# Issuing both loads of the Q and K weights from ScalarE's queue in a four-layer kernel

## The chip, the cores and the metric

The kernel runs on one core of one Trainium2 chip. The metric is the device time of one execution in microseconds (us). A core has five engines with an instruction queue each: TensorE (PE, with its weight loads as PEld), VectorE (DVE), ScalarE (ACT), GpSimd (POOL) and SyncE (SP). SyncE computes nothing; in this kernel its queue issues all transfers (DMAs).

## The reference

The input x has 2048 tokens of 512 features in bf16. Four layers follow each other, A, B, A, B, with the same weights for both A and both B. Each takes a layernorm of x and adds its result to x.

```
x = x + A(layernorm(x))      # linear attention, 32 heads of 16
x = x + B(layernorm(x))      # relu(x @ w1) @ w2, 512 -> 1376 -> 512
x = x + A(layernorm(x))
x = x + B(layernorm(x))

A:  q, k, v = x @ wqkv                      # 512 -> 3 * 512
    pq, pk = phi(q), phi(k)                 # phi(t) = (t + 1 if t > 0 else exp(t)) + 1e-6
    kv = sum over tokens of pk * v, z = sum over tokens of pk
    o = (pq @ kv) / (pq . z + 1e-6),  result = o @ wo
```

## The kernel before

The 2048 tokens are 16 tiles of 128 tokens, four tiles to a chunk. Weights and activations stay in on-chip memory; x is read once into `xin` and the result written once. Every operation is an entry of a graph (`g.add`, and `dma` for a transfer). A planner (`_list_schedule`) walks the graph with estimated costs and hand-made priorities (`HINTS`, `SEQS`) and gives each engine a fixed order. `emit_engine` then writes each engine's instructions in that order, with a semaphore wait for every dependence that is not known to be met already. A transfer is always an entry of SP's order, and the engine that needs its data waits for the transfer's own semaphore to reach 16.

What the change touches is the start of the first layer. SP's order there is:

- `ld_x0_0`: tile 0 of x, 128 KB, one run of 1 KB for each of 128 partitions (line 744)
- `ld_x0_1`: tiles 1 to 3 of x, 384 KB, one run of 3 KB for each partition (line 744)
- `ld_wqk0`: the Q and K columns of rows 0 to 255 of wqkv, 512 KB, two runs of 2 KB for each partition (line 750)
- `ld_wqk1`: the same of rows 256 to 511, 512 KB (line 750)
- `ld_x1_0` and `ld_x1_2`: tiles 4 and 5, and 6 and 7, of x, 256 KB each; the second is issued only when `ld_x0_1` has landed
- chunks 3 and 2 of x, 512 KB each, in that order; chunk 3 is issued only when `ld_wqk1` has landed

None of the first five waits for anything. PE begins with matmuls on constants (`warm`, line 775) whose results nobody reads. Tiles 0 to 3 then take a short path: VectorE computes the statistics (lines 802 and 803), subtracts the mean (line 1554), PE transposes the tile (line 883), and ScalarE or VectorE copies the transposed tile to `Tb` (lines 887 and 888). Two further statistics, those of tile 3, are made by ScalarE (lines 1564 and 1566), in front of its first copies. The K projections and the token-wise Q projections of these four tiles (line 928, `wqkv` and `Tb`) are split into a part a over rows 0 to 255, which needs `ld_wqk0`, and a part b over rows 256 to 511, which needs `ld_wqk1`. From chunk 1 on a tile is normalized on VectorE (line 845) and transposed by a DMA (line 866, `Tb<-xn`). ScalarE evaluates a projection in two passes (lines 910 and 912), VectorE finishes it (lines 914 and 921).

ScalarE's own order begins with `table` (lines 763 and 765): it loads a function table and runs a tiny activation that reads `nhalf`, which POOL sets (line 783). The function that the diff edits:

Of the kernel before, what the change touches and what calls it, by code (L numbers as in the profile page):

```python
# [606 lines left out]
def build_kernel(nc, A_x, A_wqkv, A_wo, B_w1, B_w2, out, n_layers_pairs=2, A_PE_CHUNKS=0, windows=None,  # L607
# [20 lines left out]
    with es:  # L628
# [52 lines left out]

        sem_eng = {e: es.enter_context(nc.semaphore("sem_" + e)) for e in (PE, ACT, DVE, POOL)}
        dma_sems = []

        g = _Graph()
        eng_h = {PE: nc.tensor, ACT: nc.scalar, DVE: nc.vector, POOL: nc.gpsimd, SP: nc.sync}
# [21 lines left out]
        def dma(emit, reads, writes, xfer_ns, name, issue=C_SP_ISSUE, late=0.0):  # L708
            sem = es.enter_context(nc.semaphore("dsem%d" % len(dma_sems)))
            dma_sems.append(sem)  # L710

            def _emit(eng, emit=emit, sem=sem):
                return emit(eng).then_inc(sem, 16)
            op = g.add(SP, _emit, reads, writes, dur=issue, lat=xfer_ns, dma=True, name=name)
            op.seq = sem
            op.late = late
            return op
# [25 lines left out]
        def ld_x(t, lo=0, hi=4, lat=1300.0, after=()):  # L743
            dma(lambda e: e.dma_start(xin[:, 4 * t + lo:4 * t + hi, :], tok_view(A_x, t, lo, hi)),  # L744
                list(after), [("xin", i) for i in range(4 * t + lo, 4 * t + hi)], lat, "ld_x%d_%d" % (t, lo))
# [3 lines left out]
        for k in range(2):  # L749
            dma(lambda e, k=k: e.dma_start(wqkv[:, 2 * k:2 * k + 2, 0:2 * D], wq_v[:, 2 * k:2 * k + 2, 0:2 * D]),  # L750
                [], [("wk", k), ("wq", k)], 1700.0, "ld_wqk%d" % k, late=(0.0, 300.0)[k])
# [109 lines left out]
        def transpose_chunk(t, extra_reads=(), parts=1):  # L861
            n = 4 // parts
            for k in range(parts):
                i0 = 4 * t + n * k
                lat = 2650.0 if parts == 1 else (2350.0 if k == 0 else 1050.0)
                dma(lambda e, i0=i0: e.dma_start_transpose(Tb[:, i0:i0 + n, :, :].rearrange("p i c t -> p (i c) t"),
                                                           xn[:, i0:i0 + n, :].rearrange("p i d -> p (i d)")),
                    [("xn", i) for i in range(i0, i0 + n)] + list(extra_reads),
                    [("T", i) for i in range(i0, i0 + n)], lat, "tr%d_%d" % (t, k), issue=1300.0)
# [946 lines left out]
        def emit_engine(e, handle):  # L1816
            for o in order[e]:
                for d in waits[o.idx]:
                    if d.dma:
                        handle.wait_ge(d.seq, 16)  # L1820
                    else:
                        handle.wait_ge(sem_eng[d.eng], d.seq)  # L1822
                ins = o.emit(handle)
                if not o.dma:
                    ins.then_inc(sem_eng[e], 1)
            if e == SP:
                for o in final_waits:
                    handle.wait_ge(o.seq, 16)

        with nc.Block() as block:  # L1830
            @block.tensor
            def _(t):
                emit_engine(PE, t)

            @block.scalar
            def _(s):
                emit_engine(ACT, s)

            @block.vector
            def _(v):  # L1840
                emit_engine(DVE, v)

            @block.gpsimd
            def _(p):
                emit_engine(POOL, p)

            @block.sync
            def _(sp):
                emit_engine(SP, sp)
# [3 lines left out]
def bass_interleave_layers__linear_attn_block__dense_activation_relu__prompt_kernel(  # L1853
    nc: bass.Bass,
    A_x: bass.AP,
    A_wqkv: bass.AP,
    A_wo: bass.AP,
    B_x: bass.AP,
    B_w1: bass.AP,
    B_w2: bass.AP,  # L1860
    out: bass.AP,
):
    build_kernel(nc, A_x, A_wqkv, A_wo, B_w1, B_w2, out)
# [28 lines left out]
```

## Time and profile before

| | |
|---|---|
| median of 3 runs | 267.29 us (267.24 to 267.83) |
| the profiled execution | 267.75 us |
| its span, first to last instruction | 266.0 us |
| granted TensorE clock, mean | 1.000 |
| PE busy | 260.9 us, 98% of the span |
| DVE, ACT, POOL busy | 215.4, 192.0, 51.2 us |
| DMA queues | one for data (q1), two for instructions |

The page of the profile gives one execution. Times of instructions are in us from the start of the span; the span leaves out some 1.75 us that the measured time of that execution has around it. A timeline row has the start, the length, the engine, the line, the operation, output and input, the count of merged instructions, and in brackets the idle time before the first of them with what ended it.

### The profile page before, as it was taken

The numbers are of one execution on the slowest core, as the hardware profiler recorded it, in microseconds if no ns is written. First come the engines' busy times: TensorE is split into PE (matmuls) and PEld (weight loads), VectorE is DVE, ScalarE is ACT, GpSimd is POOL, SyncE is SP. The second block draws the span as 40 slices with busy tenths as digits, with TensorE's granted clock in tenths as the row PEclk, the third lists the DMA queues.
The fourth block names the chain that finished last, engine by engine and source line by source line (L and its number), as shares of the span: only waits on it lengthen the run. The fifth ranks groups of instructions, "written<-read, shape, count | busy, mean of one in ns | idle before, by whom it ended". The sixth has DMA issues, their size and how long they took to land.

```text
span 266.0 us, 5120 instructions
## 1 busy us (share of the span) xinstructions
PE 260.9 (98%) x1890; PEld 171.2 (64%) x1890; DVE 215.4 (81%) x557; ACT 192.0 (72%) x420; POOL 51.2 (19%) x131
## 2 busy tenths in 40 slices
PE   7999999999999999999999999999999999999996
PEld 3344444644755888767776744474488888888874
DVE  4897986799889999879786848479999888697865
ACT  4798899998975756898718689578599974656300
POOL 6410010012860023400001340001734040000000
PEclk9999999999999999999999999999999999999999
DMA  6744489866249023150000313054460501602104
GB/s 213 252 88 81 139 159 366 229 156 100 44 87 160 0 21 58 25 99 1 2 0 0 66 27 68 4 140 111 107 120 2 99 2 38 140 2 70 52 1 160
DMA packets 48122, 23.22 MB, mean 87 GB/s; under 512 B 38784, under 2 KB 45920, under 8 KB 48096
## 3 DMA queue, kind: packets, MB, share of 16 engines
q1 hardware_dynamic: 48096, 22.88, 37.2%
q8 instruction: 15, 0.25, 0.4%
q14 instruction: 11, 0.09, 0.1%
HBM read 7.14 MB, written 2.10 MB: 35 GB/s over the span
## 4 chain that ended last, share of the span: by engine, by line
PE 91%; DMA 4%; DVE 3%; SPq 1%; issue 0%; DVEq 0%
PE ps L928 91%; DMA xin<-in_A_x_dram 3%; DMA Tb<-xn 1%; DVE bst L802 1%; DVE big L921 1%; DVE xn L845 0%; DVE wqkv L944 0%; SPq L750 0%; SPq L744 0%; DVE escr L914 0%; DVE xn L1610 0%; DVE mv L803 0%; DVE veps L809 0%; DVEq L1822 0%
## 5 line engine op out<-in xcount | busy, mean ns | idle before, releaser
L928 PE MATMUL ps<-Tb,w 128*128 128x256 f16 (+2 forms) x240 | 42.0, 301 | 0.0
L1327 ACT ACTIVATE big<-ps 128x512 bf16<-128x512 f32 x58 | 33.0, 597 | 10.3 <-PE ps L928 10.0
L960 ACT ACTIVATE sqscr<-xres 128x512 bf16<-128x512 f32 x48 | 29.9, 626 | 9.6 <-DVE xres L954 9.4
L928 PE MATMUL ps<-w,big 128*128 128x256 bf16 (+5 forms) x213 | 36.5, 293 | 0.0
L928 PE MATMUL ps<-wqkv,Tb 128*128 128x512 bf16 x144 | 34.5, 379 | 0.9 <-DMA wqkv<-in_A_wqkv_dram 0.6
L928 PE MATMUL ps<-big,xn 128*128 128x512 bf16 (+1 forms) x160 | 31.2, 336 | 0.2 <-DVE veps L809 0.2
L910 ACT ACTIVATE big<-ps 128x512 bf16<-128x512 f32 x48 | 28.7, 603 | 1.5 <-PE ps L928 1.4
L928 PEld LDWEIGHTS ps<-Tb,w 128*128 128x128 f16 (+1 forms) x240 | 23.2, 98 | 9.3
L928 PE MATMUL ps<-xn,xin 128*128 128x256 f16 x168 | 28.8, 272 | 0.0
L1274 DVE TENSOR_TENSOR ps<-ps,escr 128x256 f32<-128x256 f32 x56 | 22.8, 427 | 7.1 <-PE ps L928 6.6
L912 ACT ACTIVATE escr<-ps 128x512 bf16<-128x512 f32 x44 | 25.7, 604 | 3.4 <-PE ps L928 3.3
L928 PE MATMUL ps<-Tb,wqkv 128*128 128x512 bf16 x112 | 27.1, 379 | 0.0
L825 POOL TENSOR_SCALAR mean<-s 128x4 f32<-128x4 f32 (+1 forms) x13 | 3.7, 285 | 117.4 <-DVE xres L954 117.3
L928 PE MATMUL ps<-Mf,big 128*128 128x512 bf16 x112 | 25.0, 379 | 0.0
L928 PEld LDWEIGHTS ps<-wqkv,Tb 128*128 128x128 bf16 x144 | 13.7, 98 | 16.5 <-DMA wqkv<-in_A_wqkv_dram 1.1
L928 PEld LDWEIGHTS ps<-w,big 128*128 128x128 bf16 (+1 forms) x213 | 20.3, 98 | 5.2
L928 PEld LDWEIGHTS ps<-big,xn 128*128 128x128 bf16 x160 | 15.1, 98 | 12.1 <-POOL xn L979 0.7
L928 PE MATMUL ps<-xin,big 128*128 128x256 bf16 x150 | 20.8, 272 | 0.0
L914 DVE TENSOR_SCALAR escr<-escr 128x512 bf16<-128x512 bf16 x52 | 14.3, 286 | 6.7 <-ACT escr L912 6.5
L928 PEld LDWEIGHTS ps<-Mf,big 128*128 128x128 bf16 x112 | 10.7, 98 | 12.7 <-DVE big L1105 0.3
L921 DVE TENSOR_TENSOR big<-big,escr 128x512 bf16<-128x512 bf16 x46 | 18.4, 417 | 0.2
L928 PEld LDWEIGHTS ps<-Tb,wqkv 128*128 128x128 bf16 x112 | 10.8, 98 | 11.7 <-issue 0.4
(139 smaller groups left out, 499.4 us busy)
## 6 DMA issues: line engine op xcount, KB each, us to landing
big<-rdc SPq DMA_DIRECT2D x32, 128.0 KB, 2.7
wqkv<-in_A_wqkv_dram SPq DMA_DIRECT2D x3, 512.0 KB, 5.0
w<-in_B_w_dram SPq DMA_DIRECT2D x1, 1376.0 KB, 7.6
w<-in_B_w_dram SPq DMA_DIRECT2D x1, 1280.0 KB, 10.8
xin<-in_A_x_dram SPq DMA_DIRECT2D x2, 512.0 KB, 4.5
out_dram<-wqkv SPq DMA_DIRECT2D x2, 512.0 KB, 3.5
xin<-in_A_x_dram SPq DMA_DIRECT2D x2, 256.0 KB, 6.2
wo<-in_A_wo_dram SPq DMA_DIRECT2D x1, 512.0 KB, 7.6
```

The lines of the kernel that those rows point to most:

```text
L802: g.add(DVE, lambda e: e.bn_stats(bst[:, i, :], xin[:, i, :]), [("xin", i)] + list(after), [("bst", i)], C_DVE_BNST, name="bnst%d" % i)
L825: g.add(POOL, lambda e: e.tensor_scalar(mean[:, sl], s1[:, sl], -INV_D, None, ALU.mult), [("s1", i) for i in tl], [("mean", i) for i in tl ...
L910: g.add(ACT, lambda e: e.activation(dst_ap, psv[:, b, :], ACTF.Identity, bias=1.0 + 1e-6, scale=sc), [("ps", b)] + rk, [dst_key], C_ACT_PS ...
L912: g.add(ACT, lambda e: e.activation(esc, psv[:, b, :], ACTF.Exp, scale=sc), [("ps", b)] + rk, [ekey], C_ACT_EXP + xd, name=name + "_exp")
L914: g.add(DVE, lambda e: e.tensor_scalar(esc, esc, 1.0, 1e-6, ALU.min, ALU.add), [ekey], [ekey], C_DVE_BF4X, name=name + "_em")
L921: g.add(DVE, lambda e: e.tensor_tensor(dst_ap, dst_ap, esc, ALU.max), [dst_key, ekey], [dst_key], 340.0, name=name + "_phi")
L928: last = e.matmul(o, l, r, start=st, stop=sp, skip_group_check=skip)
L960: g.add(ACT, lambda e: e.activation(sqscr[:, q, :], xres[:, i, :], ACTF.Square, accum_out=s2[:, i:i + 1]), [("xres", i)], [("sqscr", q), ( ...
L1274: g.add(DVE, lambda e: e.tensor_tensor(psv[:, bank, 256:512], psv[:, Y, 0:256], m5, ALU.add), [("ps", Y), ("escr", s)], [("ps", bank)], C_ ...
L1327: g.add_flex([(ACT, lambda e: e.activation(unit_ap(u), psv[:, b, :], ACTF.Relu), C_ACT_PSUM), (DVE, lambda e: e.tensor_scalar(unit_ap(u), ...
```

## The change

`ld_wqk0` and `ld_wqk1` stay in SP's order as entries that emit no instruction. Their two DMA instructions are written at the head of ScalarE's queue, in front of its function table load. Each still increments its own semaphore, so whoever waits for the weights does so as before, and so do SP's later loads. The order of every engine's other operations is unchanged.

```diff
--- before.py
+++ after.py
@@ -681,6 +681,8 @@
         dma_sems = []
+        ACT_LOADS = ('ld_wqk0', 'ld_wqk1')
+        act_loads = []
 
@@ -711,6 +713,9 @@
             def _emit(eng, emit=emit, sem=sem):
                 return emit(eng).then_inc(sem, 16)
+            if g.layer == 0 and name in ACT_LOADS:
+                act_loads.append((ACT_LOADS.index(name), _emit))
+                _emit = lambda eng: None
             op = g.add(SP, _emit, reads, writes, dur=issue, lat=xfer_ns, dma=True, name=name)
@@ -1834,6 +1839,8 @@
             @block.scalar
             def _(s):
+                for _, load in sorted(act_loads, key=lambda a: a[0]):
+                    load(s)
                 emit_engine(ACT, s)
```

## The prediction

> **What bounds the kernel now.** I read the page first, then the waits of PE, then the first 20 us of each queue's timeline, since the change touches nothing later.
>
> ```profile
> span 266.0 us, 5120 instructions
> PE 260.9 (98%) x1890; PEld 171.2 (64%) x1890; DVE 215.4 (81%) x557; ACT 192.0 (72%) x420; POOL 51.2 (19%) x131
> ...
> PE ps L775 <- PEq L1877: 0.8, 1, 0.8
> PE ps L883 <- DVE xn L1554: 0.6, 1, 0.6
> PE ps L928 <- DMA wqkv<-in_A_wqkv_dram: 0.6, 1, 0.6
> PE ps L928 <- DMA Tb<-xn: 0.3, 1, 0.3
> PE ps L928 <- DVE veps L809: 0.2, 1, 0.2
> ```
>
> PE is the bound, and the five rows are all of its waits in the whole execution. Where they lie, the timelines show; first PE, then DVE:
>
> ```profile
> 0.83 3.78 PE L775 MATMUL ps<-const-bfloat16-1.0 128*128 128x512 bf16 x9 [0.83 <-PEq L1877]
> 4.41 0.42 PE L883 MATMUL ps<-ident,xn 128*128 128x128 bf16 x2
> ...
> 6.01 0.40 PE L883 MATMUL ps<-ident,xn 128*128 128x128 bf16 x4 [0.63 <-DVE xn L1554]
> ...
> 7.77 0.59 PE L928 MATMUL ps<-wqkv,Tb 128*128 128x512 bf16 x2
> 8.96 5.79 PE L928 MATMUL ps<-wqkv,Tb 128*128 128x512 bf16 x26 [0.60 <-DMA wqkv<-in_A_wqkv_dram]
> 14.95 3.19 PE L928 MATMUL ps<-big,xn 128*128 128x512 bf16 x16 [0.20 <-DVE veps L809]
> ...
> 20.65 1.90 PE L928 MATMUL ps<-wqkv,Tb 128*128 128x512 bf16 x8 [0.35 <-DMA Tb<-xn]
> ...
> 2.88 0.69 DVE L802 BATCH_NORM_STATS2 bst<-xin 128x6 f32<-128x512 bf16 x1 [2.88 <-DMA xin<-in_A_x_dram]
> ...
> 4.66 0.70 DVE L802 BATCH_NORM_STATS2 bst<-xin 128x6 f32<-128x512 bf16 x1 [0.47 <-DMA xin<-in_A_x_dram]
> ...
> 7.99 0.42 DVE L888 COPY Tb<-ps 128x512 bf16<-128x512 bf16 x1
> 9.58 1.29 DVE L802 BATCH_NORM_STATS2 bst<-xin 128x6 f32<-128x512 bf16 x2 [1.18 <-DMA xin<-in_A_x_dram]
> ```
>
> After the warm-up, which reads no data, PE works on tiles 0 to 3, waits 0.60 us for the second half of the weights at 8.96, and then 0.20 and 0.35 us more, at 14.95 and 20.65. The last two are fed by the normalization of chunk 1, which starts at 9.58, when VectorE has stood idle for 1.18 us for `ld_x1_0`. So two landings hold the start back, the weights' at 8.96 and chunk 1's at 9.56; behind 20.65 PE never waits. The chain of work that ended last goes the second way: SP's issues, one behind the other, then that load, VectorE, the DMA transpose, and PE for 242 us.
>
> ```profile
> 1.71 0.43 SPq L750
> 2.13 0.04 issue
> 2.18 0.47 SPq L750
> 2.65 0.04 issue
> 2.69 6.87 DMA xin<-in_A_x_dram
> ...
> 16.75 3.86 DMA Tb<-xn
> 20.61 0.05 issue
> 20.65 242.27 PE ps L928 x1790
> ```
>
> **What the edit moves.** Two issues of 0.43 and 0.47 us leave SP's queue, and with their gaps `ld_x1_0` is issued 0.98 us earlier, at about 1.71. SP's issue of `ld_x1_2` hangs on `ld_x0_1`, and chunk 3 and then chunk 2 on `ld_wqk1`; these follow their releasers, and nothing near the start waits for them. On ScalarE the two issues come first:
>
> ```profile
> 0.79 0.87 SPq L744 DMA_DIRECT2D xin<-in_A_x_dram  x2
> ...
> 2.62 1.28 ACT L763 ACT_TABLE_LOAD   x1 [2.62 <-POOL nhalf L783]
> 3.92 0.20 ACT L765 ACTIVATE lnw<-nhalf 128x2 f32<-128x2 f32 x1
> 4.66 0.63 ACT L1564 ACTIVATE sqscr<-xin 128x512 bf16<-128x512 bf16 x1 [0.54 <-DMA xin<-in_A_x_dram]
> ```
>
> If ScalarE's queue starts like SP's, at 0.79, the 0.90 us of issues end at 1.7, and the table load waits for POOL until 2.62 anyway: cost nothing. Without that cover there is still the 0.54 us in front of 4.66. `ld_wqk1` is issued at some 1.26 instead of 2.18, 0.92 us earlier; `ld_wqk0` also 0.92.
>
> **The price.** The first x loads had the transfer engines to themselves for their first microsecond; now the weights start beside them. The windows of one microsecond (PE, PEld, DVE, ACT and POOL busy, PE clock, DMA share, GB/s):
>
> ```profile
> 1.00:2.00 1.00, 1.00 (x3) 0.29 (x2) 0.00 (x0) 0.00 (x0) 0.94 (x2) 1.00 0.15 44
> 2.00:3.00 1.00, 1.00 (x4) 0.38 (x3) 0.12 (x1) 0.38 (x1) 0.60 (x3) 1.00 1.02 225
> 3.00:4.00 1.00, 1.00 (x4) 0.35 (x3) 0.93 (x3) 0.99 (x2) 0.12 (x1) 1.00 1.05 290
> 4.00:5.00 1.00, 1.00 (x7) 0.61 (x6) 0.53 (x2) 0.46 (x2) 1.00 (x3) 1.00 0.78 272
> ...
> 6.00:7.00 1.00, 0.99 (x11) 0.67 (x11) 0.97 (x3) 0.81 (x4) 0.84 (x4) 1.00 0.99 381
> 7.00:8.00 1.00, 1.00 (x9) 0.50 (x8) 0.96 (x5) 0.81 (x3) 0.91 (x4) 1.00 1.00 387
> ```
>
> Call D the delay of `ld_x0_1`, on whose landing both VectorE and ScalarE start at 4.66. By 4.65 44 + 225 + 290 + 0.65 x 272 = 736 KB had moved. The two x loads are 128 and 384 KB, 524 thousand bytes; the other 212 KB were weights already. At the full rate of 384 KB per us (the last two rows), the 2.65 us from 2.0 to 4.65 could have moved 1018 KB and moved 692, so 326 KB were spare. No run here shows two load queues side by side (all data went by one), so I bound D:
> - None: if the weights only fill the spare capacity.
> - 0.81 us: if the two queues take turns run by run and nothing spare can be used. The x loads have 256 runs (one per partition and load), `ld_wqk0` has 256, so all of it, 524 KB, goes ahead of the last x run, 312 KB more than now, over 384.
> - 1.24 us: if besides that the two queues issue one at a time, so that `ld_x0_1` waits for one issue of 0.43.
> - 2.18 us: if all 1049 KB of weights go first, (1049 - 212) / 384.
>
> I take 0.6, the middle of the first and the third. The dips at 225 to 290 GB/s are those of loads that have just begun and would in part recur. Tile 0 may be delayed as much; its short chain had 0.47 us of slack in front of 4.66, so D decides.
>
> On the arbitration the Trainium skill ("DMA: Bandwidth & Descriptors", section on queues, rings and completion order) says that each transfer engine serves its queues in turn, a packet at a time, which would give about the second value; no run here shows it yet. The same page ("Issuing engines are not separate DMA queues") speaks against the edit: several issuing engines save only the time to issue. The 0.90 us of the rows above is that time, and the transfer rate is no higher.
>
> **The sum.** PE's work on tiles 0 to 3 and everything up to 8.96 shifts by D; the waits of 0.60 + 0.20 + 0.35 = 1.15 us go. Shift of the end: 0.6 - 1.15 = -0.55. The same through VectorE: it is done with the first tiles at 8.41, now 9.01, and starts chunk 1 at 9.01 in place of 9.58, 0.57 earlier; the feeds of 14.95 and 20.65 come that much earlier. That needs `ld_x1_0` landed by 9.01 (9.56 less 0.98 of issue is 8.58) and `ld_wqk1` by about 8.80: the two matmuls at 7.77 take 0.22 us each, 5.79 over 26, so PE is ready at 8.20 plus D. It is there at 8.96 now, and comes at about 8.0 if the transfers follow the issue. Both hold with half a microsecond or so to spare; they are what is late next. A lead of PE survives behind 20.65, where ScalarE too waits for PE:
>
> ```profile
> 21.73 0.60 ACT L910 ACTIVATE big<-ps 128x512 bf16<-128x512 f32 x1 [0.44 <-PE ps L928]
> ```
>
> The profiled execution took 267.75 us, 1.75 beyond its span, and 0.46 above the median of the three runs, 267.29. Against its own time the sum gives 267.20, against the median 266.7, which I forecast.
>
> **The rivals.** One of them needs a row of the first 9.5 us by line and shape (busy time, mean ns of one):
>
> ```profile
> L775 PE MATMUL ps<-const-bfloat16-1.0 128*128 128x512 bf16 x8 | 3.6, 625 | 0.8 <-PEq L1877 0.8
> ```
>
> - A larger gain: D near zero. For it speaks the spare 326 KB against 312 KB needed; against it, the dips. -1.15 us: 266.1.
> - No change: D of 0.9 to 1.6, because the two queues' issues exclude each other and share what is left; -0.25 to +0.45 us, about 267.4. For it: even the plain alternation gives 0.81. The Trainium skill ("Perfetto Trace Analysis", the DMA instruction on HWDGE) has one descriptor generator, locked by one queue at a time, and would give the third value of D, near 267.4; no run here shows whether ScalarE's issues are held up by SP's.
> - Slower, by the weights first: they are the older or longer work on each transfer engine and x comes behind them, D = 2.18, shift +1.03, 268.3. It decides against the edit from D = 1.15 on. For it: x has only 128 KB queued when the weights' 512 KB arrive. Against: SP's first issue is no later than ScalarE's.
> - Slower, by a cold PE: the warm-up ends at 4.61, and the first transpose, at 4.41 now, comes D or more later, so PE stands idle for over half a microsecond where it now runs through. The eight warm-up matmuls of 512 columns took 3.6 us, 0.45 each, and those behind 8.96 take 0.22, so PE starts at half speed and speeds up only after some 4 us of work. If the gap puts this off by a few microseconds, the eight projections up to 8.4 cost 8 x 0.23 = 1.84 more, the 16 transposes at twice their cost some 0.9; 0.63 of it goes into the wait at 6.01. 0.6 + 2.1 - 1.15 = +1.55, half that much extra +0.5; I price it at +1.0, 268.3. Against it: over 3.5 us of unbroken warm-up stay as they were. By the Trainium skill ("TensorE: Matmul & The Clock Gate", Part 1) the clock rises after a busy window of about 3.4 us; by that the warm-up nearly suffices alone, if the window lies well.
>
> **How the numbers follow.** The forecast's case, D of 0.3 to 0.9 and so -0.85 to -0.25 us, gets 0.40; the larger gain 0.12; no change 0.14; weights first 0.16; the cold PE 0.18. What a measurement of this kernel can tell from no change is about 0.2%, 0.53 us. Of the forecast's case 0.26 lies beyond that and 0.14 within; of no change 0.10 lies within and 0.04 is slower when a landing is late besides. Faster: 0.26 + 0.12 = 0.38. Same: 0.14 + 0.10 = 0.24. Slower: 0.16 + 0.18 + 0.04 = 0.38. The range goes from 266.1, the larger gain, to 268.4, just past the price of both slow cases; it leaves out the long tails of these two, somewhat under 0.2. The forecast's own range is 266.4 to 267.0.
>
> **What would show it.** Right: a second data queue in the profile; the weights' issues at the head of ScalarE's queue, before 1.8; VectorE's first statistics later than 2.88 and its second at about 5.3; no wait of PE at the second half of the weights, which begins at about 8.8; no wait of VectorE for `ld_x1_0`; PE's 0.20 and 0.35 gone, and the long stretch of PE beginning near 20.1. Wrong: second statistics at 6 or later (weights first); transposes spaced twice as far and projections at 0.45 us behind 5 us (cold PE); issues of ScalarE and SP that alternate (one generator); or waits of PE for `wqkv` or `Tb` as long as before.

## The result, and the profile after

| | before | after |
|---|---|---|
| median | 267.70 us of 9 executions (267.10 to 268.44) | 269.51 us of 9 executions (268.28 to 271.01) |
| ratio, 95% interval | | 1.0072 (1.0055 to 1.0089) |
| the profiled execution, its span | 267.75, 266.0 us | 269.59, 267.9 us |

The change makes the kernel slower by 0.72%; the medians differ by 1.8 us. The kernel before has 267.70 here and had 267.29 in the three runs ahead of the prediction, so 0.4 us of the distance to the forecast is that of the base. The page of the profile after (span 267.9 us), its line of busy times, PE's waits and the two data queues (packets, MB, share of the transfer engines' span):

```profile
PE 261.9 (98%) x1890; PEld 172.0 (64%) x1890; DVE 215.6 (80%) x557; ACT 191.8 (72%) x420; POOL 50.9 (19%) x131
...
q1 hardware_dynamic: 47552, 21.83, 35.9%
q10 hardware_dynamic: 544, 1.05, 1.2%
...
PE ps L888 <- DVE xn L1559: 2.3, 1, 2.3
...
PE ps L933 <- DMA Tb<-xn: 0.3, 1, 0.3
```

All lines stand five higher than before (L928 is L933 now). The waits for `wqkv` and for `veps` are gone, as intended. In their place stands one wait of 2.3 us for a normalized tile, and PE is busy 1.0 us longer with the same 1890 instructions. The timelines of ScalarE, VectorE and PE:

```profile
0.79 0.99 ACTq L755 DMA_DIRECT2D wqkv<-in_A_wqkv_dram  x2
2.62 1.28 ACT L768 ACT_TABLE_LOAD   x1 [2.62 <-POOL nhalf L788]
...
3.06 0.69 DVE L807 BATCH_NORM_STATS2 bst<-xin 128x6 f32<-128x512 bf16 x1 [3.06 <-DMA xin<-in_A_x_dram]
6.12 0.69 DVE L807 BATCH_NORM_STATS2 bst<-xin 128x6 f32<-128x512 bf16 x1 [1.76 <-DMA xin<-in_A_x_dram]
10.90 0.42 DVE L893 COPY Tb<-ps 128x512 bf16<-128x512 bf16 x1 [1.36 <-PE ps L888]
...
7.48 0.60 PE L888 MATMUL ps<-ident,xn 128*128 128x128 bf16 x4 [2.33 <-DVE xn L1559]
8.52 1.91 PE L933 MATMUL ps<-wqkv,Tb 128*128 128x512 bf16 x4
```

ScalarE's two issues are done at 1.78 and cost its table load nothing. Tile 0's statistics begin 0.18 us later than before (3.06 against 2.88). Those of tile 1, which need `ld_x0_1`, begin at 6.12 in place of 4.66: 1.46 us later. PE then stands idle from 5.15 to 7.48. Its first four projections at 8.52 take 1.91 us in all. The same four of before took 1.13:

```profile
6.58 1.13 PE L928 MATMUL ps<-wqkv,Tb 128*128 128x512 bf16 x4
```

The windows of after (columns as in the prediction) show why:

```profile
6.00:7.00 1.00, 0.00 (x0) 0.00 (x0) 0.84 (x2) 0.88 (x3) 0.00 (x0) 1.00 1.00 389
7.00:8.00 1.00, 0.52 (x5) 0.52 (x6) 0.96 (x4) 0.72 (x3) 0.80 (x2) 0.74 0.92 316
8.00:9.00 1.00, 1.00 (x8) 0.66 (x7) 0.93 (x4) 0.88 (x3) 0.83 (x5) 0.50 0.15 55
10.00:11.00 1.00, 1.00 (x8) 0.59 (x6) 0.10 (x1) 0.00 (x0) 0.18 (x1) 0.55 0.87 336
```

The granted clock, full since 4.08, falls to 0.50 at 7.50 and is back at 10.91, 3.4 us after each. Ahead of 4.08 the trace has no entry of the clock, and the view prints 1.00 there, as in the prediction's rows; that PE starts at half speed shows in the length of its matmuls alone. For the same reason the mean granted clock of an execution leaves out a late first rise (it is 1.000 for one below whose clock rises at 9.81). The clock at half explains the projections' length and VectorE's wait of 1.36 for PE at 10.90. The chain that ended last names the late load, and where PE's unbroken stretch begins:

```profile
1.25 4.85 DMA xin<-in_A_x_dram
...
22.49 242.27 PE ps L933 x1790
```

The stretch is 242.27 us long in before as well and begins 1.84 us later than there (20.65). The times of the two executions differ by 1.84 too. So here all of the loss arises before 22.5 us, and from here on I follow that beginning, called S.

### The profile page after: what moved, and what is told of

Read it like the earlier page. It is cut to its first block, busy times and chain, and to the rows that moved or that the text cites. A ratio compares the mean times of both kernels' runs of the same rounds, so it can differ in the third digit from the quotient of the medians.

```text
span 267.9 us, 5120 instructions
## 1 busy us (share of the span) xinstructions
PE 261.9 (98%) x1890; PEld 172.0 (64%) x1890; DVE 215.6 (80%) x557; ACT 191.8 (72%) x420; POOL 50.9 (19%) x131
## 4 chain that ended last, share of the span: by engine, by line
PE 92%; DMA 3%; DVE 2%; ACT 1%; issue 0%; SPq 0%; DVEq 0%
PE ps L933 91%; DMA xin<-in_A_x_dram 2%; DMA Tb<-xn 1%; PE ps L888 1%; DVE bst L807 0%; DVE xn L850 0%; ACT big L915 0%; DVE big L926 0%; DVE wqkv L949 0%; DVE escr L919 0%; ACT escr L917 0%; SPq L749 0%; DVE xn L1559 0%; DVE mv L808 0%; DVE xn L1615 0%
## 5 line engine op out<-in xcount | busy, mean ns | idle before, releaser
L933 PE MATMUL ps<-Tb,w 128*128 128x256 f16 (+2 forms) x240 | 42.0, 301 | 0.0
L933 PE MATMUL ps<-w,big 128*128 128x256 bf16 (+5 forms) x213 | 36.5, 293 | 0.0
L933 PE MATMUL ps<-wqkv,Tb 128*128 128x512 bf16 x144 | 35.2, 387 | 0.3 <-DMA Tb<-xn 0.3
L933 PE MATMUL ps<-big,xn 128*128 128x512 bf16 (+1 forms) x160 | 31.2, 336 | 0.0
L933 PEld LDWEIGHTS ps<-Tb,w 128*128 128x128 f16 (+1 forms) x240 | 23.1, 98 | 9.3
L933 PE MATMUL ps<-xn,xin 128*128 128x256 f16 x168 | 28.8, 272 | 0.0
L933 PE MATMUL ps<-Tb,wqkv 128*128 128x512 bf16 x112 | 27.1, 379 | 0.0
L933 PE MATMUL ps<-Mf,big 128*128 128x512 bf16 x112 | 25.0, 379 | 0.0
L933 PEld LDWEIGHTS ps<-wqkv,Tb 128*128 128x128 bf16 x144 | 14.2, 100 | 15.8 <-DMA Tb<-xn 0.6
L933 PEld LDWEIGHTS ps<-w,big 128*128 128x128 bf16 (+1 forms) x213 | 20.3, 98 | 5.2
L933 PEld LDWEIGHTS ps<-big,xn 128*128 128x128 bf16 x160 | 15.2, 98 | 11.7 <-issue 0.7
L933 PE MATMUL ps<-xin,big 128*128 128x256 bf16 x150 | 20.8, 272 | 0.0
L933 PEld LDWEIGHTS ps<-Mf,big 128*128 128x128 bf16 x112 | 10.7, 97 | 12.7 <-DVE big L1110 0.3
L933 PEld LDWEIGHTS ps<-Tb,wqkv 128*128 128x128 bf16 x112 | 10.8, 98 | 11.7 <-issue 0.4
```

The source lines that it names most:

```text
L933: last = e.matmul(o, l, r, start=st, stop=sp, skip_group_check=skip)
```

## The experiments

The reading above gives two joint causes: the weights' first load, issued before `ld_x0_1`, is served ahead of it, and the gap that this makes on PE lets the clock fall. Rivals: that the second queue itself costs, whatever the order; that the clock alone costs; that the gain expected was there only in the one execution profiled. What follows from each run is told by mechanism, not by the letters that some expectations use.

**The same order of loads from one queue.** Before, with `ld_wqk0` in front of `ld_x0_1` on SP's queue; ScalarE issues nothing:

```diff
+        order[SP][1], order[SP][2] = order[SP][2], order[SP][1]
```

> The kernel before, all loads from SP's queue, with only the issues of the second load of x and the first weights' load exchanged (x tile 0, weights 0, x tiles 1 to 3, weights 1). Theory A (what matters is which transfer goes first, not which queue issues it): the second load of x lands at 6.1 to 6.5 us in place of 4.65, PE is idle for 2 us or more in front of tile 2, the clock falls as in the changed kernel, and the time is 1.5 to 2.5 us over the kernel before. Rival B (the second queue itself is what costs, by its ring or its issue): less than 0.7 us over the kernel before, the delay less the waits that go.

269.98 us, ratio 1.0081 (1.0062 to 1.0099). Timelines of SP's queue, VectorE and PE:

```profile
1.25 0.41 SPq L750 DMA_DIRECT2D wqkv<-in_A_wqkv_dram  x1
1.71 0.46 SPq L744 DMA_DIRECT2D xin<-in_A_x_dram  x1
...
5.99 0.69 DVE L802 BATCH_NORM_STATS2 bst<-xin 128x6 f32<-128x512 bf16 x1 [1.64 <-DMA xin<-in_A_x_dram]
7.35 0.40 PE L883 MATMUL ps<-ident,xn 128*128 128x128 bf16 x4 [2.17 <-DVE xn L1554]
22.40 1.90 PE L928 MATMUL ps<-wqkv,Tb 128*128 128x512 bf16 x8 [0.32 <-DMA Tb<-xn]
```

One queue with that order does what the change does with two: `ld_x0_1` at 5.99, a wait of 2.17, S at 22.40. In five of the six executions the mean granted clock is 0.993 or 0.994. The order is enough for the whole loss, and the second queue isn't needed for it.

**Half of the change.** Only `ld_wqk0` goes to the head of ScalarE's queue:

```diff
-        ACT_LOADS = ('ld_wqk0', 'ld_wqk1')
+        ACT_LOADS = ('ld_wqk0',)
```

> Half of the change: only the first weights' load is the first instruction of ScalarE's queue, the second stays on SP's queue at 1.71 us behind the second load of x. Theory A (loads are served whole in the order of issue): the first weights' load, issued at 0.79, is ahead of the second load of x, which lands at 5.6 to 6.2 as in the changed kernel, and the time is that of the changed kernel, 1 to 2 us over the kernel before. Rival B (both weights' loads crowd x out together): the second load of x lands by 5.2 and the time is within 0.5 us of the kernel before.

269.82 us, ratio 1.0072 (1.0049 to 1.0095): all of the loss. The profiled execution is one of the shorter ones, 268.42. Timelines of VectorE and PE, and PE's busy time in the 3.41 us behind the rise of the clock:

```profile
6.00 0.69 DVE L807 BATCH_NORM_STATS2 bst<-xin 128x6 f32<-128x512 bf16 x1 [1.53 <-DMA xin<-in_A_x_dram]
7.92 1.12 PE L933 MATMUL ps<-wqkv,Tb 128*128 128x512 bf16 x4
21.02 1.90 PE L933 MATMUL ps<-wqkv,Tb 128*128 128x512 bf16 x8 [0.53 <-DMA Tb<-xn]
...
5.81:9.22 3.41, 1.87 (x18) 1.17 (x19) 3.08 (x9) 2.97 (x8) 1.98 (x7) 1.00 0.92 299
```

Here `ld_x0_1` is as late as in the swap, but the clock rose only at 5.81 and kept its height, and S is 21.02 in place of 22.40. So by this one profile the late load alone costs some 0.7 us (21.0 against 20.3, the mean of three profiles of before, below) and the fall of the clock 1.3 to 1.4 more. The six executions fall apart accordingly: 268.05 and 268.42 with a mean granted clock of 1.000, and four of 269.75 to 269.96, three of them with 0.994 (the fourth has 1.000).

**The gap filled.** The change, with eight (then five) more warm-up matmuls of 512 columns in front of tile 2's transposes. A second line, not shown, holds the planner's estimate of that entry at its old value:

```diff
-                warm([256], "warm%d" % k)
+                warm([256] + ([512] * 8 if k == 5 else []), "warm%d" % k)
```

> The changed kernel, with eight warm-up matmuls of 512 columns on constants more in front of tile 2's transposes, where PE stood idle from 5.15 to 7.48 us. Theory A (two costs: the first weights' load goes ahead of the second load of x, which lands 1.46 us later than before; and PE's idle stretch lets the granted clock fall to 0.50 from 7.5 to 10.9 us): the loads land as in the changed kernel (VectorE's second statistics at about 6.1 us), the clock stays at 1.00, and only the delay less the waits that go is left, 0.3 to 0.5 us over the kernel before, about 1.5 us under the changed kernel. Rival B (the clock costs nothing here, the late load alone makes the 1.8 us): no faster than the changed kernel, 1.5 to 2 us over the kernel before.

> The changed kernel with five (instead of the eight of the first experiment) warm-up matmuls of 512 columns more in front of tile 2's transposes. At half speed they take 5 x 0.43 = 2.1 us and at full speed 1.1, so they end before the late tile arrives in either case. Theory A (PE's idle stretch costs through the clock, in those executions in which the clock's window falls on it; the eight of before also delayed PE where the clock was still low, and moved a code fetch onto a DMA transpose): the time falls below the changed kernel's 269.5 to some 268.0 to 268.8, and no execution shows a mean clock of 0.994. Rival B (the clock is not what spreads the changed kernel's times): 269.3 or more, as with eight.

269.31 us, ratio 1.0068 (1.0047 to 1.0089), with eight; 268.98, 1.0060 (1.0041 to 1.0078), with five. PE's timeline with eight:

```profile
20.57 1.90 PE L933 MATMUL ps<-wqkv,Tb 128*128 128x512 bf16 x8 [0.33 <-DMA Tb<-xn]
68.10 1.70 PE L933 MATMUL ps<-Tb,w 128*128 128x256 bf16 x13 [0.83 <-DMA Tb<-xn]
```

and with five:

```profile
20.98 1.90 PE L933 MATMUL ps<-wqkv,Tb 128*128 128x512 bf16 x8 [0.33 <-DMA Tb<-xn]
68.37 0.83 PE L933 MATMUL ps<-Tb,w 128*128 128x256 bf16 x6 [0.70 <-DMA Tb<-xn]
```

At the start both do what the clock's part demands: it stays up (in none of the twelve executions is its mean below 0.999), and S is 20.57 and 20.98, though `ld_x0_1` comes at 5.71 and 6.14. But the time follows only in part. By its median the first fits the rival, that the clock costs nothing; the second lies between the two forecasts. Both profiled executions have a wait that before and after don't have, 0.83 and 0.70 us for a DMA transpose near 68. That is about half of the 1.75 us by which the first one's median exceeds before's, and its profiled execution, 268.75, is the shortest of six; what the longer ones, up to 270.36, had is not on record. Two fetches of instructions, on q8 and q14, lie in that stretch. The DMA queues (packets, MB, share of the transfer engines' time) of the eight-matmul kernel from 65 to 66 us:

```profile
q14 instruction: 1, 0.01, 10.6%
q8 instruction: 1, 0.02, 5.8%
```

and of before, from 65 to 66 and from 68 to 69:

```profile
q14 instruction: 1, 0.01, 3.1%
...
q8 instruction: 1, 0.02, 5.7%
```

With the extra PE instructions both fetches fall into the microsecond in which the chunk's two transposes are under way, and these land 5.6 us after their issue (the mean of the two) in place of 3.6. In before the larger fetch comes when they have landed. I read the wait as the fetches' from where they lie; no run takes them away, so this is not shown. The medians can't price the clock, but the beginnings of the stretch do.

**A cold start without the change.** Before, with one of the eight leading warm-up matmuls of 512 columns (the ninth, of 256, stays, so two of nine are left):

```diff
-                    for n in cols:
+                    for n in cols[-1:]:
```

> The kernel before with one of its nine leading warm-up matmuls instead of nine (PE idle until the first transpose at about 4.2 us); all loads as before. Theory A (PE's clock follows its activity, and with the kernel's first projections at half speed the start of PE's unbroken stretch moves): projections near 7 us take 0.43 each instead of 0.22, the unbroken stretch begins at 21.5 to 23 us in place of 20.65, and the time is 1 to 2.5 us over the kernel before, with no transfer changed. Rival B (the clock costs nothing, only late loads do): within 0.3 us of the kernel before.

268.75 us, ratio 1.0052 (1.0032 to 1.0072). VectorE and PE:

```profile
4.79 0.69 DVE L802 BATCH_NORM_STATS2 bst<-xin 128x6 f32<-128x512 bf16 x1 [0.52 <-DMA xin<-in_A_x_dram]
7.19 1.91 PE L928 MATMUL ps<-wqkv,Tb 128*128 128x512 bf16 x4
21.40 1.90 PE L928 MATMUL ps<-wqkv,Tb 128*128 128x512 bf16 x8 [0.51 <-DMA Tb<-xn]
```

The loads are issued as in before, the first four projections take 1.91 us, as at half speed in after, until the clock rises at 9.68, and S is 21.40, 1.1 later than the mean of before; the time is longer by 1.33. That prices a clock at half by itself, near the 1.3 to 1.4 of half the change.

**The issues held back.** The change, with ScalarE's issues behind a wait for POOL's second operation, so that `ld_x0_1` is issued first:

```diff
+                s.wait_ge(sem_eng[POOL], 2)
                 for _, load in sorted(act_loads, key=lambda a: a[0]):
```

> The changed kernel, with ScalarE's two issues held until POOL has done its second operation, about 1.35 us, that is just behind SP's second issue at 1.25. Theory A1 (transfers are served in the order of their issue over both queues): the second load of x lands by 4.8 us as before; the weights are issued about 0.3 us earlier than in the kernel before and the load of tiles 4 and 5 0.9 us earlier; 0.3 to 0.6 us faster than the kernel before. Rival A2 (the two queues take turns run by run whatever the order of issue): the second load of x lands 0.6 us or more late, at 5.3 or later, and the time is within 0.3 us of the kernel before or over it.

267.90 us, ratio 1.0031 (1.0006 to 1.0057). The issues, VectorE and PE:

```profile
1.39 0.95 ACTq L755 DMA_DIRECT2D wqkv<-in_A_wqkv_dram  x2
4.27 0.69 DVE L807 BATCH_NORM_STATS2 bst<-xin 128x6 f32<-128x512 bf16 x1
7.41 1.04 PE L933 MATMUL ps<-wqkv,Tb 128*128 128x512 bf16 x4 [0.62 <-DMA wqkv<-in_A_wqkv_dram]
20.21 1.90 PE L933 MATMUL ps<-wqkv,Tb 128*128 128x512 bf16 x8 [0.31 <-DMA Tb<-xn]
```

Issued 0.6 us later the weights take nothing from `ld_x0_1`, which is there by 4.27, with both queues in use. But now the first half of the weights is late, by 0.62 us, and S is 20.21: no gain, though both issues precede the 1.71 and 2.18 of before's SP queue. Seven of the twelve executions took 266.95 to 267.97, five took 269.53 to 270.17. Three of the five have a mean granted clock of 0.994, two have 1.000; none of the seven is below 0.999. So the fall of the clock happens here too, and what the other two had isn't on record.

**Held back, and the first half only.** `ld_wqk0` alone from ScalarE, with the same wait; `ld_wqk1` from SP:

```diff
-        ACT_LOADS = ('ld_wqk0', 'ld_wqk1')
+        ACT_LOADS = ('ld_wqk0',)
@@
+                s.wait_ge(sem_eng[POOL], 2)
```

> The kernel before with only the first weights' load moved to ScalarE's queue and held there until POOL's second operation, so that it is issued at about 1.39 us; the second weights' load stays on SP's queue, at 1.71. The order of the five first loads by time of issue is that of the kernel before, each from the third on issued 0.3 to 0.5 us earlier. Theory A (loads are served whole in the order of their issue, over both queues): the second load of x lands at 4.3 to 4.7, PE has no idle stretch over 0.7 us, no execution is slowed by the clock, and the time is 0.2 to 0.5 us below the kernel before. Rival B (the two queues share the transfer engines whatever the order): the second load of x lands 0.4 us or more late and the time is at or above the kernel before.

267.60 us, ratio 1.0006 (0.9995 to 1.0016): no difference, where 0.2 to 0.5 us of gain were forecast; the clock falls in no execution. PE:

```profile
7.03 1.04 PE L933 MATMUL ps<-wqkv,Tb 128*128 128x512 bf16 x4 [0.43 <-DMA wqkv<-in_A_wqkv_dram]
19.86 1.90 PE L933 MATMUL ps<-wqkv,Tb 128*128 128x512 bf16 x8 [0.33 <-DMA Tb<-xn]
```

The order of before is kept, and the two halves of the weights are issued at 1.39 and 1.71 in place of 1.71 and 2.18. The second half is there in time, but the first is not: it lands at about 7.0, later than in any profile of before (6.8 at the latest, below). PE waits 0.43 us for it, and S is 19.86, where a repeat of before has 19.93. What lies behind PE's stretch took 3.6 us here and 3.1 in the first profile of before, so the early S didn't reach the end.

**The other load moved.** Before, with only `ld_x0_1` from ScalarE:

```diff
-        ACT_LOADS = ('ld_wqk0', 'ld_wqk1')
+        ACT_LOADS = ('ld_x0_1',)
```

> The kernel before, with only the second load of x (tiles 1 to 3) issued from ScalarE's queue as its first instruction; the weights stay on SP's queue, now at 1.25 and 1.71 us. Theory A (the transfer that is issued first is served first, and a second queue is only a second place to issue from): that load is issued at 0.79 in place of 1.25 and lands at about 4.2, the weights and tiles 4 and 5 come 0.4 us earlier too, and the end is 0.3 to 0.5 us earlier than in the kernel before. Rival B (loads on two queues disturb each other whichever they are): the first or the second load of x lands no earlier than before, 2.88 and 4.65, and nothing is gained.

268.08 us, ratio 1.0032 (1.0012 to 1.0052). The issues, VectorE and PE:

```profile
0.78 0.40 ACTq L749 DMA_DIRECT2D xin<-in_A_x_dram  x1
0.79 0.40 SPq L749 DMA_DIRECT2D xin<-in_A_x_dram  x1
4.42 0.70 DVE L807 BATCH_NORM_STATS2 bst<-xin 128x6 f32<-128x512 bf16 x1 [4.42 <-DMA xin<-in_A_x_dram]
5.78 0.40 PE L888 MATMUL ps<-ident,xn 128*128 128x128 bf16 x2 [1.16 <-DVE xn L1559]
```

The forecast gain missed. Issued side by side, the 384 KB of `ld_x0_1` push tile 0's 128 KB from 2.88 to 4.42; PE waits 1.16 us, and the clock rises only at 9.81. S is 21.89 in this execution, 269.60, one of the longer of twelve (267.17 to 269.91).

**Both kernels profiled again.**

> The kernel before again, for a profile of another execution. Theory C (the waits that the sum took from the one profile, 0.60 us for the second weights' load and 1.18 for tiles 4 and 5, were mostly one late transfer engine of that execution): the second weights' load lands by about 8.0 in place of 8.93, PE waits 0.2 us or less for it, and PE's unbroken stretch begins 0.2 to 0.5 us before 20.65. Rival D (the waits belong to the kernel): 0.5 to 0.7 us of PE's wait again, and a stretch that begins at 20.5 to 20.8.

> The kernel before once more. Theory C and rival D as for the other look at it: a second weights' load at about 8.0 and a stretch from 20.2 to 20.4 by C, at about 8.9 and from 20.5 to 20.8 by D.

> The changed kernel again, for a profile of another execution. Theory A: the second load of x lands at 5.6 to 6.2 us whatever the execution; PE's unbroken stretch begins at 20.9 to 21.2 and the time is 268.0 to 268.7 where the granted clock stays at 1.00, and at 22.3 to 22.6 with 269.3 to 270.2 where it falls to 0.50 or rises late. Rival B (the late load alone makes the loss): a stretch from 22.3 on in every execution.

> The changed kernel once more. Theory A and rival B as for the other look at it: with the clock at 1.00 throughout, a stretch from 20.9 to 21.2 by A and from 22.3 on by B; with the clock at 0.50 for a while, 22.3 to 22.6 by both.

Before took 268.04 and 267.32 us in these, after 269.28 and 269.27. PE's timeline of the first repeat of before, and then of the second:

```profile
6.81 1.04 PE L928 MATMUL ps<-wqkv,Tb 128*128 128x512 bf16 x4 [0.32 <-DMA wqkv<-in_A_wqkv_dram]
20.33 1.90 PE L928 MATMUL ps<-wqkv,Tb 128*128 128x512 bf16 x8 [0.34 <-DMA Tb<-xn]
```

```profile
8.21 5.79 PE L928 MATMUL ps<-wqkv,Tb 128*128 128x512 bf16 x26 [0.30 <-DMA wqkv<-in_A_wqkv_dram]
19.93 1.90 PE L928 MATMUL ps<-wqkv,Tb 128*128 128x512 bf16 x8 [0.37 <-DMA Tb<-xn]
```

The wait for the weights is 0.30 and 0.32 us, half of the 0.60 on which the sum stood, once for the first half and once for the second. S is 20.33 and 19.93 against 20.65: the execution that I argued from was the latest of three. Its time is not the longest, though. PE's stretch is 242.27 us in all three, but behind it, where VectorE finishes and the last results are stored, come 3.1 us in the first profile and 3.6 and 3.4 in the repeats. So a few tenths of a gain at S need not show in the time. One repeat of after, VectorE and PE:

```profile
5.77 0.70 DVE L807 BATCH_NORM_STATS2 bst<-xin 128x6 f32<-128x512 bf16 x1 [1.53 <-DMA xin<-in_A_x_dram]
22.19 1.90 PE L933 MATMUL ps<-wqkv,Tb 128*128 128x512 bf16 x8 [0.33 <-DMA Tb<-xn]
```

The other has 5.75 and 22.16. Both have the clock at 0.50 for 3.4 us, as the first had, so the two repeats can't tell the late load's part from the clock's. The three beginnings average 22.28 for after and 20.30 for before; with half the change's 21.02 between them the difference of 1.98 splits into 0.7 for the late load and 1.3 for the clock. The spans average 267.65 and 265.95, 1.7 apart.

The mean granted clock of the executions that were only timed agrees. Of the nine of after four have 0.993 or 0.994 and took 269.51 to 270.17; of the five with 1.000 three took 268.28 to 268.55 and two 269.33 and 271.01, which stay unexplained (a late first rise would not show in the mean). Of the 42 executions of before that were timed along with the experiments none is below 0.998, and none took more than 268.27. So the median of after is an execution in which the clock fell; of the five others three lost 0.6 to 0.9 against the 267.70.

## Why the prediction was wrong, point by point

I forecast 266.7 us and a gain; the kernel lost 1.8 and lies beyond the range's 268.4.

**What held.** ScalarE's issues are hidden by the wait for POOL, at the times given. SP's and ScalarE's first issues both start at 0.79 and take 0.40 and 0.47 us, so the engines don't exclude each other. PE's waits for the weights and at 14.95 are gone, and VectorE's for `ld_x1_0` too. The loss sits where the sum looked for the gain, in front of PE's long stretch.

**D, the delay of `ld_x0_1`.** Taken as 0.6, it measured 1.46 in the profiled executions, and by the means of three 1.45 (5.88 against 4.43). The step that failed is the middle of the first and the third bound. The weights don't fill spare capacity, and here the queues don't take turns. The DMA queues of after from 2.5 to 3.5 us:

```profile
q10 hardware_dynamic: 105, 0.22, 94.1%
q1 hardware_dynamic: 26, 0.01, 4.7%
```

The weights' queue has 94.1% of the transfer time. The 26 packets of q1 are all under 2 KB, so none is one of the 3 KB runs of `ld_x0_1`, which was issued at 1.25; its data come in bulk only from 4 us on. The Trainium skill ("DMA: Bandwidth & Descriptors", section on queues, rings and completion order) has each transfer engine serve its queues in turn, a packet at a time. These rows don't look like that: the first weights' load goes ahead of a load that was issued 0.46 us later on the other queue. The trace also has the time at which each of the sixteen parts of a load signalled its landing. Those of `ld_wqk0` came from 4.23 to 5.11, those of `ld_x0_1` each some 0.98 later, from 5.21 to 6.10, so a part of x waited for the whole part of the weights. The fourth bound, 2.18, was the right mechanism with one of the two loads: the second, issued at 1.3 beside `ld_x0_1`, landed two microseconds behind it, 6.8 us after its issue. Half of the 1049 KB is 524 KB, over 384 an estimate of 1.37, near the measured 1.46. Taking off the 212 KB that were weights by 4.65 gives the 0.81 of the second bound, and that was too much: in before the parts of `ld_x0_1` landed from 3.88 to 4.63, and the weights moved behind the early ones, not ahead of it.

Issued at the same time, the two queues do look like turns. With `ld_x0_1` moved to ScalarE (q10) beside tile 0 on SP (q1), from 2.0 to 3.5 us:

```profile
q10 hardware_dynamic: 113, 0.35, 65.2%
q1 hardware_dynamic: 109, 0.11, 23.8%
```

The packet counts are nearly equal, and the small load pays for it with 1.54 us. So the case of the second bound exists, but not with the lead that the change gives the weights.

**The 1.15 us that were to go.** They came from one execution. Fifteen of the sixteen parts of `ld_wqk1` had landed there by 7.85, and PE, ready at 8.36, waited for the last, at 8.92; of `ld_x1_0` fifteen came by 8.49 and the last at 9.55. In the repeats the wait for the weights was half, and S up to 0.7 earlier. Of the three terms the 0.35 was never removable: PE waits 0.3 to 0.5 for `Tb` at S in every kernel shown here, after included. And even with D at nothing (`ld_x0_1` at 4.27 and 4.51) the loads held back showed no gain; the first half of the weights, issued earlier, landed later.

**The clock.** The rival of a cold PE was named with 0.18 and 268.3, and it is the larger part of the loss; the sum itself put the clock at nothing, where it costs 1.3. Its working counts eight projections up to 8.4, where before's timeline has six. Two more things were wrong with it. It stood as an alternative to the weights first, while the one brings about the other, and the two prices add. And its mechanism was a late rise, argued against by 3.5 us of unbroken warm-up. The warm-up did suffice, the clock rose at 4.08 (in before at 4.96), and fell again one window later, in which PE had been busy for only 1.07 us:

```profile
4.08:7.50 3.42, 1.07 (x10) 0.50 (x9) 1.59 (x5) 1.42 (x5) 1.53 (x4) 1.00 1.02 392
```

The Trainium skill ("TensorE: Matmul & The Clock Gate", Part 1) states a free-running window of about 3.4 us; with 3.42 and 3.41 between rise, fall and rise the trace agrees. In before the window behind the rise has 2.77 us of PE, and the clock stays. That the busy time decides rests on these windows and on the gap filled, where 2.19 and 3.41 us kept it up.

## What to carry to other kernels

A load that is issued earlier from another engine's queue is not an addition: here it went ahead of a load issued 0.46 us after it, from the same queue or another, so ask first which small load the first computation hangs on, and keep that one in front. A gap of two microseconds on PE soon after its clock has risen can cost twice, by itself and by the clock at half speed for a further window. And a wait of half a microsecond in front of a long unbroken stretch should be seen in more than one profile of the kernel before it is counted as a gain.

## What the runs showed of the hardware that I had not expected

- **The clock's windows have a phase of their own.** In the executions profiled it rose for the first time anywhere from 3.98 to 6.58 us (behind a cut warm-up or an early gap at 9.68 and 9.81), and what followed went with PE's busy time in the next 3.41 us: it fell after 1.07, 1.36, 1.33 and 1.25 us busy (after, its repeats, the swap), and stayed after 1.87, 2.19 and 2.77 (half the change, five matmuls, before). Where the limit lies between 1.36 and 1.87 no run tells. To rise takes more: a window with 2.26 us (the other load moved, 2.98 to 6.40) left it low. That one kernel's executions fall into two groups fits this, but the phase of executions that were not profiled isn't known.
- **Code fetches move with the instruction count.** Eight or five more matmuls at 5 us brought a wait of 0.83 or 0.70 us at 68, where two fetches now lie beside DMA transposes that took 5.6 and 5.4 us instead of 3.6. That the fetches are the cause isn't shown.
- **A wait can hang on one part of a load in sixteen.** In before the last part of `ld_wqk1` landed 1.07 us behind the fifteenth, and PE's 0.60 us hung on it.
- **Still open:** the rule by which two data queues are served. With issues at the same time the packets took turns, and with a lead of 0.46 us the first load went ahead part by part. With 0.32 (held back, the first half only) five parts of the first half landed by 5.88 and eleven from 6.51 to 6.99, those of the second half from 6.97 to 7.73, so the halves were mostly served side by side. With both halves held back fourteen parts of the first landed by 5.74 and two at 6.82 and 7.36; why these two lag isn't known.
